# Moving five stores of one batch into the next batch's first product, and the last two stores to another queue

## The chip, the cores and the metric

The kernel runs on one core of one Trainium2 chip. A time is device microseconds of one execution of the whole program, lower is better. The engines of the core are TensorE (matrix products), VectorE, ScalarE, GpSimd and SyncE. SyncE computes nothing here: it only asks for transfers (DMA), as ScalarE and GpSimd also can. Each of these has a queue of its own, worked off in the program's order, and all transfers are carried out by the same 16 DMA engines.

## The reference

Attention with a window and a few sink positions, and behind it a two-part MLP with residuals, for 4 batches of 768 positions:

```python
scores = scale * q @ k.T            # 8 heads of 64; kept: 4 sinks and a causal window of 128
x = softmax(scores) @ v             # heads put side by side: (4, 768, 512)
a1 = alpha1 * x + beta1
u  = x + lam * (w_tok @ a1)         # w_tok mixes the 768 positions
a2 = alpha2 * u + beta2
out = u + lam * (relu(a2 @ w_ch1) @ w_ch2)      # 512 -> 2048 -> 512, float32 out
```

## The kernel before

The positions of a batch are cut into six blocks of 128 rows, called rows 0 to 5 here; a block of 128 x 512 float32 is 256 KB. For each batch the kernel does the attention, the product with `w_tok` (`tok`), a transpose of `u` to float16 by DMA (`uTx`, L919), scale and shift on the transposed halves (L884, L886), the first product with `w_ch1` (`mlp1`, matmuls at L940 and the relu at L946 on ScalarE or L948 on VectorE), and the second product. In batches 1 to 3 the second product is seven half-width products P1 to P7 (`prod`, matmuls at L1057) whose results are added into the rows of `x` by VectorE and GpSimd (L1070, L1088, L1093, L1096). `h_sums` (L998 to L1001) makes their operands.

When the last sum of a row is done, `store` (request at L1076) sends it to the output. In batches 1 and 2 a row goes in one store of 256 KB: rows 3 to 5 after P5, rows 0 to 2 after P3. In batch 3, the last, rows 0 to 2 go in two stores of half the columns, the first half after P2 and the second after P3; rows 3 to 5 go whole.

```python
def store(p, bx, ti, cols, after):
    n_ = (cols.stop - cols.start) // 64
    add(p, {SP: 520, ACT: 550}, lambda e: queue[e].dma_start(out[b, ti * P : (ti + 1) * P, cols], row(bx)[:, cols]),
        after, [bx], lands=(8, 12 * n_ if n_ == 8 else 60))
```

The work is a list of numbered tasks. `add` makes a task; its costs in braces name the engines that may do it. Nothing is planned when the program is built: `emit` goes through `ORDER`, a list of all task numbers, takes each task's engine from the string `ENGINES` (one digit per task: 0 ScalarE, 1 VectorE, 2 TensorE, 3 GpSimd, 4 SyncE), and its buffers from `HOMES`. So `ORDER` is the order of the program, and an engine does its own tasks in that order. An engine runs ahead of the others as far as its data allows: a task's place in `ORDER` only says what it stands behind on its own engine's queue. Requests for transfers of ScalarE and SyncE share eight completion semaphores, which are handed out in turn; a request waits until the one eight before it in the program, which had the same semaphore, has landed. At the end SyncE waits for all transfers (L1329), and the engines meet in a closing barrier. No buffer of batch 2's rows is used again after its store.

The stores from batch 2's end on, in the order of the program:

| Task | Batch, row, columns | Queue | Request before, us |
|---|---|---|---|
| 870 | 2, row 5, all | ScalarE | 217.1 |
| 1093 | 3, row 1, first half | SyncE | 234.0 |
| 864 | 2, row 4, all | SyncE | 234.4 |
| 867 | 2, row 0, all | SyncE | 234.9 |
| 861 | 2, row 3, all | ScalarE | 238.9 |
| 1127 | 3, row 3, all | ScalarE | 245.0 |
| 1088 | 3, row 0, first half | ScalarE | 245.4 |
| 1136 | 3, row 5, all | SyncE | 245.4 |
| 873 | 2, row 1, all | SyncE | 245.7 |
| 876 | 2, row 2, all | SyncE | 246.3 |
| 1096 | 3, row 2, first half | SyncE | 246.8 |
| 1142 | 3, row 2, second half | ScalarE | 247.2 |
| 1130 | 3, row 4, all | ScalarE | 247.6 |
| 1133 | 3, row 0, second half | SyncE | 248.0 |
| 1139 | 3, row 1, second half | SyncE | 249.0 |

Of the kernel before, what the change touches and what calls it, by code (L numbers as in the profile page):

```python
# [77 lines left out]
def kernel(  # L78
# [119 lines left out]
    for r in range(NR):  # L198
# [91 lines left out]
    )  # L290
    ENGINES = (
        "3313134433443333444444444444444433334443111211211212021212021203331121211210210200201210"
# [5 lines left out]
        "2121202111202021202120202011202121212121111121212121212121132111213121421021421421421044"  # L298
        "4400004440443333330404040404040404020201012120101212133201012121312030121213120101212133"
        "2032121312121312104210421040001210421042104000121212120212121212121202120202021202121202"  # L300
        "0202020112120202020212020112021212121211111212121212121213121112131210214214210214214044"
        "4404404404433333304040404043404040202010121203012121312010121213320103212131203012121312"
        "0321213321213121042104210410002104213421341010202021202120212120212020202020212020212120"
        "202020112020212021202020112020210202142141111212121212121211121112131210210214214214210"
    )
    HOMES = (
        "145602340010102001213310200221013302203140101100511203013044215120821000003331a501103130"
# [1026 lines left out]
```

## Time and profile before

| What | Value |
|---|---|
| Median of 3 runs | 254.4 us (254.31 to 255.53) |
| The profiled execution's own time | 254.82 us |
| Its span, first to last instruction | 252.9 us |
| TensorE busy | 245.7 us, 97% of the span |
| VectorE, ScalarE, GpSimd busy | 193.4, 131.4, 107.4 us |
| Mean granted TensorE clock | 0.995 |
| Store requests at L1076 | 13 on SyncE, 8 on ScalarE |

An engine's busy time is a share of the span, an average over stages with different limits. Asking for a transfer is not counted as busy; a row for requests (SPq for SyncE's queue, ACTq for ScalarE's) gives the time of the request itself in ns as smallest, median and largest, and the line on landing gives us from the start of the request until the data has arrived. The profile's rows name a tile without its number, so all rows of all batches are `x`.

### The profile page before, as it was taken

What the parts mean: (1) busy time and instruction counts of PE and PEld (TensorE: products, weight loads), DVE (VectorE), ACT (ScalarE), POOL (GpSimd) and SP (SyncE); (2) the same over time, 40 slices, a digit from 0 to 9 for tenths busy, and PEclk for the clock granted to TensorE, in tenths of its full rate; (3) what the DMA queues carried; (4) which work ended last, traced back from release to release, by engine and by line L of the source; (5) the groups of instructions that cost most, each with busy time, mean ns of one, the idle gap of its engine ahead of it and who ended that gap; (6) DMA issues with size and microseconds to landing.
All of it is one profiled execution on the core that took longest, in us unless ns stands there. A gap on an engine that the chain in (4) does not pass through costs nothing.

```text
span 252.9 us, 5512 instructions
## 1 busy us (share of the span) xinstructions
PE 245.7 (97%) x2167; PEld 160.7 (64%) x2167; DVE 193.4 (76%) x401; ACT 131.4 (52%) x218; POOL 107.4 (42%) x126
## 2 busy tenths in 40 slices
PE   8899999999999999999999999999999999999992
PEld 8654655675555444566777776577577676667882
DVE  6798987778788976688889995677789985039882
ACT  2389935688986025687741435556650234643000
POOL 8618734987866516442772040066562130000010
PEclk9999999999999999999999999999999999999998
DMA  7999999999999997896489274320000131100317
GB/s 214 201 234 292 263 204 306 359 355 285 219 209 231 211 196 166 166 259 141 108 177 178 52 156 128 124 65 0 3 0 3 32 72 23 41 0 3 137 54 268
DMA packets 86129, 38.79 MB, mean 153 GB/s; under 512 B 73540, under 2 KB 80460, under 8 KB 86104
## 3 DMA queue, kind: packets, MB, share of 16 engines
q1 hardware_dynamic: 67120, 28.85, 48.4%
q10 hardware_dynamic: 15240, 6.32, 10.5%
q0 software_dynamic: 3744, 3.28, 8.2%
q8 instruction: 17, 0.28, 0.5%
q14 instruction: 8, 0.07, 0.1%
HBM read 29.91 MB, written 6.29 MB: 143 GB/s over the span
## 4 chain that ended last, share of the span: by engine, by line
PE 90%; ACT 4%; DVE 3%; issue 2%; DVEq 0%; ACTq 0%
PE h L940 32%; PE P L1057 22%; PE tok L860 12%; PE ch L1125 8%; PE pv L726 4%; PE S L625 4%; PE idle L148 2%; PE tp L515 1%; ACT wt L822 1%; ACT E L647 1%; DVE qkT L157 1%; PE S L620 1%; PE tp L512 1%; PE pv L719 1%; DVE lb_b L1175 1%
## 5 line engine op out<-in xcount | busy, mean ns | idle before, releaser
L940 PE MATMUL h<-uT,w1f 128*128 128x384 f16 x512 | 89.3, 326 | 0.1
L940 PEld LDWEIGHTS <-w1f 128*128 128x128 f16 x512 | 48.4, 98 | 31.9 <-issue 2.0
L946 ACT ACTIVATE hT<-h 128x384 f16<-128x384 f32 x77 | 36.7, 492 | 34.4 <-PE h L940 30.6
L948 DVE TENSOR_SCALAR hT<-h 128x384 f16<-128x384 f32 x51 | 27.3, 551 | 23.7 <-PE h L940 23.3
L1057 PEld LDWEIGHTS <-hT 128*128 128x128 f16 x408 | 39.3, 98 | 7.1 <-DVE hT L1000 0.7
L647 ACT ACTIVATE E<-S 128x1024 f16<-128x1024 f32 (+1 forms) x39 | 37.8, 1002 | 6.7 <-PE S L625 5.7
L770 POOL TENSOR_TENSOR tm<-x,la_b 128x512 f32<-128x512 f32 x18 | 24.7, 1372 | 22.2 <-DVE xh L773 12.0
L860 PE MATMUL tok<-xh,wtokT 128*128 128x512 f16 x144 | 33.2, 379 | 0.0
L1057 PE MATMUL P<-w2f,hT 128*128 128x256 f16 x216 | 26.8, 273 | 0.0
L155 ACT CAST u<-x 128x512 f16<-128x512 f32 x17 | 10.3, 616 | 27.3 <-DVE x L867 26.2
L1093 POOL TENSOR_TENSOR x<-x,pt 128x256 f32<-128x256 f32 x4 | 3.9, 963 | 46.0 <-DVE pt L1088 46.0
L1070 DVE TENSOR_TENSOR x<-x,P 128x256 f32<-128x256 f32 x45 | 18.0, 416 | 6.9 <-PE P L1057 6.1
L1057 PE MATMUL P<-w2s,hT 128*128 128x256 f16 x192 | 23.3, 273 | 0.0
L860 PEld LDWEIGHTS <-wtokT 128*128 128x128 f16 x144 | 13.8, 98 | 14.7 <-issue 0.2
L1125 PE MATMUL ch<-w2f,hT 128*128 128x512 f16 x96 | 22.7, 379 | 0.0
L752 DVE TENSOR_TENSOR x<-pv,rec 128x256 f32<-128x256 f32 x48 | 20.4, 424 | 1.6
L155 ACT CAST n<-nat 128x768 f16<-128x768 f32 x20 | 16.2, 830 | 9.2 <-DVE w2s L972 7.2
L867 DVE TENSOR_TENSOR x<-x,tok 128x512 f32<-128x512 f32 x24 | 16.0, 681 | 4.6 <-PE tok L860 4.3
L726 PEld LDWEIGHTS <-E 128*128 128x128 f16 x328 | 15.2, 97 | 4.9 <-issue 1.1
L726 PE MATMUL pv<-vfs,E 128*128 128x65 f16 x328 | 17.7, 194 | 0.0
L587 POOL TENSOR_SCALAR_AFFINE_SELECT E<-E 128x512 f16<-128x512 f16 x12 | 8.8, 756 | 17.9 <-ACT E L647 17.9
L157 POOL CAST vfs<-vnat 128x512 f16<-128x512 f32 x18 | 13.5, 755 | 4.2 <-PE pv L726 4.2
(133 smaller groups left out, 340.2 us busy)
## 6 DMA issues: line engine op xcount, KB each, us to landing
wst_w<-in_moe_w_ch_dram SPq DMA_DIRECT2D x8, 512.0 KB, 7.2
nat<-in_q_dram SPq DMA_DIRECT2D x10, 384.0 KB, 4.5
nat<-in_k_dram SPq DMA_DIRECT2D x10, 384.0 KB, 7.6
vnat<-in_v_dram SPq DMA_DIRECT2D x14, 256.0 KB, 6.2
out_dram<-x SPq DMA_DIRECT2D x11, 256.0 KB, 3.0
out_dram<-x ACTq DMA_DIRECT2D x10, 256.0 KB, 4.0
wtn<-in_moe_w_tok_dram SPq DMA_DIRECT2D x6, 384.0 KB, 6.1
w1f<-in_moe_w_ch_dram POOLq DMA_DIRECT2D x4, 512.0 KB, 10.7
```

The costliest lines, as they stand in the source:

```text
L155: nc.scalar.copy(o, i)
L647: nc.scalar.activation(eT.t, pS.t[:, :, 0 : n * w].rearrange("p e (i w) -> p e i w", i=n), AF.Exp, scale=scale)
L726: nc.tensor.matmul(po.t[:, hl, :], eT.t[:, e_, off + i, c : c + P], vf[j][:, h, :], start=(r < 2 and n == 0), stop=(n == len(parts) - 1 an ...
L752: nc.vector.tensor_mul(bx.t[:, 4 * G : 4 * G + 4, :], po.t[:, :, 0:D], rec.t.to_broadcast([P, 4, D]))
L770: engine[e].tensor_mul(bt.t, bx.t.rearrange("p h d -> p (h d)"), la1_b)
L860: nc.tensor.matmul(bank(), wtokT[:, si, ti * P : (ti + 1) * P], hs[si].t, start=(si == 0), stop=(si == NR - 1))
L940: nc.tensor.matmul(ph.t, w1f[:, c, fi * P : (fi + 1) * P], bu.t[:, c, chk * NTOK : (chk + 1) * NTOK], start=(c == 0), stop=(c == NC - 1))
L946: nc.scalar.activation(bh.t[:, fi, :], ph.t, AF.Relu)
L948: nc.vector.tensor_scalar_max(bh.t[:, fi, :], ph.t, 0.0)
L1057: nc.tensor.matmul(pc.t, hh[:, nt * P : (nt + 1) * P], w(fi), start=(first and n_ == 0), stop=(n_ == HF - 1), skip_group_check=True)
L1070: nc.vector.tensor_add(row(bx)[:, cols], row(bx)[:, cols], pc.t)
L1125: nc.tensor.matmul(pc.t, bh.t[:, fi, nt * P : (nt + 1) * P], w2f[:, fi, :], start=(fi == 0), stop=(fi == NF - 1))
```

## The change

Only `ORDER` and `ENGINES` change. Five stores of batch 2 (864, 867, 861, 873, 876) are taken out of their places among batch 3's second product and put among the tasks of batch 3's first product, around 870, which stays. In the new order the stores of batch 2 read 864, 867, 870, 861, 873, 876, all ahead of 1093. Store 861 (row 3) goes from ScalarE's queue to SyncE's. The program's last two stores, 1133 and 1139, go from SyncE's queue to ScalarE's, where they stand behind 1127, 1088, 1142 and 1130; on SyncE's queue 1093, 1136 and 1096 are left of batch 3. The order of all other tasks among themselves is the same, and so is every other engine digit.

```diff
  1006, 860, 853, 997, 868, 995, 1007, 996, 999, 865, 1008, 858, 857, 1000, 1009,
  862, 869, 866, 874, 1001, 994, 854, 1016, 863, 875, 1040, 1017, 871, 1041, 1038,
  872, 1020, 1039, 1028, 1021, 1011, 1032, 1029, 1013, 1018, 1033, 1024, 1012,
- 1019, 1034, 1010, 1042, 1035, 1025, 1036, 1076, 1037, 1043, 1070, 1077, 870,
- 1074, 1071, 1054, 1075, 1022, 1055, 1060, 1023, 1058, 1061, 1048, 1014, 1049,
- 1059, 1066, 1015, 1044, 1067, 1072, 1045, 1056, 1073, 1026, 1057, 1078, 1068,
- 1079, 1064, 1069, 1046, 1027, 1063, 1052, 1047, 1050, 1053, 1082, 1051, 1062,
- 1084, 1083, 1065, 1030, 1080, 1085, 1101, 1031, 1081, 1091, 1102, 1107, 1092,
- 1097, 1093, 1105, 1108, 864, 1098, 1103, 867, 1106, 1111, 1104, 1113, 1112,
- 1089, 1114, 1115, 1086, 1116, 1090, 861, 1094, 1087, 1109, 1099, 1121, 1100,
- 1117, 1095, 1110, 1125, 1118, 1122, 1134, 1124, 1123, 1126, 1128, 1135, 1127,
- 1088, 1119, 1136, 1120, 1140, 873, 876, 1129, 1131, 1141, 1096, 1142, 1137,
- 1130, 1132, 1133, 1138, 1139,
+ 1019, 864, 1034, 1010, 1042, 1035, 1025, 1036, 867, 1076, 1037, 1043, 1070,
+ 1077, 870, 1074, 1071, 861, 1054, 1075, 1022, 1055, 1060, 1023, 873, 1058, 1061,
+ 1048, 1014, 1049, 1059, 876, 1066, 1015, 1044, 1067, 1072, 1045, 1056, 1073,
+ 1026, 1057, 1078, 1068, 1079, 1064, 1069, 1046, 1027, 1063, 1052, 1047, 1050,
+ 1053, 1082, 1051, 1062, 1084, 1083, 1065, 1030, 1080, 1085, 1101, 1031, 1081,
+ 1091, 1102, 1107, 1092, 1097, 1093, 1105, 1108, 1098, 1103, 1106, 1111, 1104,
+ 1113, 1112, 1089, 1114, 1115, 1086, 1116, 1090, 1094, 1087, 1109, 1099, 1121,
+ 1100, 1117, 1095, 1110, 1125, 1118, 1122, 1134, 1124, 1123, 1126, 1128, 1135,
+ 1127, 1088, 1119, 1136, 1120, 1140, 1129, 1131, 1141, 1096, 1142, 1137, 1130,
+ 1132, 1133, 1138, 1139,
     )
     ENGINES = (
  "3313134433443333444444444444444433334443111211211212021212021203331121211210210200201210"
@@ -298,10 +298,10 @@
  "2121202111202021202120202011202121212121111121212121212121132111213121421021421421421044"
  "4400004440443333330404040404040404020201012120101212133201012121312030121213120101212133"
  "2032121312121312104210421040001210421042104000121212120212121212121202120202021202121202"
- "0202020112120202020212020112021212121211111212121212121213121112131210214214210214214044"
+ "0202020112120202020212020112021212121211111212121212121213121112131214214214210214214044"
  "4404404404433333304040404043404040202010121203012121312010121213320103212131203012121312"
  "0321213321213121042104210410002104213421341010202021202120212120212020202020212020212120"
- "202020112020212021202020112020210202142141111212121212121211121112131210210214214214210"
+ "202020112020212021202020112020210202142141111212121212121211121112131210210210214210210"
     )
     HOMES = (
  "145602340010102001213310200221013302203140101100511203013044215120821000003331a501103130"
```

## The prediction

> **What bounds the kernel now.** I read the page first, then the chain of waits in order of time, then the stretches of the last eight microseconds, then the stores alone.
>
> ```profile
> span 252.9 us, 5512 instructions
> ...
> PE 245.7 (97%) x2167; PEld 160.7 (64%) x2167; DVE 193.4 (76%) x401; ACT 131.4 (52%) x218; POOL 107.4 (42%) x126
> ...
> PE 90%; ACT 4%; DVE 3%; issue 2%; DVEq 0%; ACTq 0%
> ```
>
> TensorE is busy for 97% of the span. The chain of waits from 196 us on shows that in both places that the change touches nothing but TensorE is on the path:
>
> ```profile
> 210.53 18.85 PE h L940 x116
> ...
> 231.78 16.61 PE P L1057 x152
> 248.39 0.02 issue
> 248.41 0.42 DVE x L1070
> ```
>
> The chain ends with the last sum on VectorE at 248.41 + 0.42 = 248.83. The span ends at 252.9. What lies in these 4.1 us is no engine's work, so the stores must be read by themselves (the last one, then the program's closing instructions, L1329):
>
> ```profile
> L1076 SPq DMA_DIRECT2D out_dram<-x x1: 965/965/965, 249.0 to 249.0; - x1
> DMA to landing us min/median/max: 2.7/2.7/2.7
> ...
> L1329 SPq EVENT_SEMAPHORE  x11: 17/28/28, 250.0 to 252.8; - x11
> ...
> L1329 SPq DRAIN  x3: 7/7/13, 252.1 to 252.4; - x3
> ```
>
> The last store is asked for at 249.0, 0.15 us after its data, and lands 2.7 us later, at 251.7. SyncE waits for the landings one by one (11 waits from 250.0), drains at 252.1, and the span ends 1.2 us after the last landing. So the tail is: data ready 248.83, +0.15 to the request, +2.7 to the landing, +1.2 to close. Why 2.7 is in the stretches (the last two numbers of a row are the busy share of the 16 DMA engines and GB/s; the number before them is the granted clock):
>
> ```profile
> 245.00:246.00 1.00, 1.00 (x11) 0.90 (x10) 1.00 (x3) 0.00 (x0) 0.23 (x1) 1.00 0.14 49
> 246.00:247.00 1.00, 1.00 (x11) 0.90 (x10) 0.90 (x3) 0.00 (x0) 0.00 (x0) 1.00 1.03 381
> 247.00:248.00 1.00, 1.00 (x12) 0.89 (x11) 0.58 (x2) 0.00 (x0) 0.00 (x0) 1.00 1.02 361
> 248.00:249.00 1.00, 0.38 (x4) 0.09 (x1) 0.42 (x1) 0.00 (x0) 0.00 (x0) 1.00 1.03 379
> 249.00:250.00 1.00, 0.00 (x0) 0.00 (x0) 0.00 (x0) 0.00 (x0) 0.00 (x0) 1.00 1.03 349
> 250.00:251.00 1.00, 0.00 (x0) 0.00 (x0) 0.00 (x0) 0.00 (x0) 0.00 (x0) 0.73 1.04 358
> 251.00:252.00 1.00, 0.00 (x0) 0.00 (x0) 0.00 (x0) 0.00 (x0) 0.00 (x0) 0.50 0.27 90
> ```
>
> The DMA engines are full (1.02 to 1.04) from 246 to 251, at a mean of (381 + 361 + 379 + 349 + 358) / 5 = 366 GB/s. The seven rows add up to 1.97 MB, which is ten stores: five of 256 KB (0.262 MB) and five of half a row (0.131 MB). Two of the five large ones are batch 2's rows 1 and 2. The last store's data waits behind a backlog. Without one, a 256 KB store looks like this (the store of batch 2's row 3, asked for at 238.9 with nothing else in flight):
>
> ```profile
> L1076 ACTq DMA_DIRECT2D out_dram<-x x1: 338/338/338, 238.9 to 238.9; - x1
> DMA to landing us min/median/max: 2.0/2.0/2.0
> ...
> 239.50:240.50 1.00, 1.00 (x12) 0.90 (x10) 0.74 (x2) 0.00 (x0) 0.00 (x0) 1.00 0.70 262
> ```
>
> It lands after 2.0 us, of which its data takes 0.7. Half of the data takes 0.131 / 0.366 = 0.36 us less, so I estimate 1.65 us for a half store on free engines.
>
> **The change, part one: five stores of batch 2 move forward.** In the tail this removes two of SyncE's requests (rows 1 and 2, 0.524 MB) from in front of the last stores. At 366 GB/s that is 1.43 us of backlog. Not all of it can be had, since the last store's data is not ready before 248.83. What is left, 1.44 MB: the first four stores (0.79 MB) are through at about 245.9 + 2.1 = 248.0, and the other four are asked for from 247.2 on, about as fast as they move. The last landing time therefore falls from 2.7 towards 1.65: a gain between 0.7 (if it lands as the lone 256 KB store, 2.0) and 1.05. The other three, rows 4 and 0 (asked for from 234.4 on) and row 3 (238.9), leave stretches in which nobody waits for them: nothing there.
>
> Where they go: SyncE's queue holds six transposes up to 206.24 + 2.51 = 208.75 and then nothing until 234.0, so the five run there as soon as their sums are done, before the place in the program at which they stand.
>
> ```profile
> 206.24 2.51 SPq L919 DMA_TRANSPOSE uT<-u  x2
> ...
> 208.60 0.75 DVE L1070 TENSOR_TENSOR x<-x,P 128x256 f32<-128x256 f32 x2
> 210.57 0.42 DVE L1070 TENSOR_TENSOR x<-x,P 128x256 f32<-128x256 f32 x1 [1.22 <-PE P L1057]
> 212.26 1.29 ACT L884 ACTIVATE uT<-uT,ab 128x384 f16<-128x384 f16 x2
> 214.40 0.37 DVE L886 TENSOR_SCALAR uT<-uT,ab 128x384 f16<-128x384 f16 x1
> ...
> 209.00:209.75 0.75, 0.75 (x8) 0.52 (x6) 0.35 (x2) 0.54 (x2) 0.00 (x0) 1.00 0.59 113
> 209.75:210.50 0.75, 0.75 (x9) 0.65 (x7) 0.00 (x0) 0.44 (x1) 0.00 (x0) 1.00 0.00 0
> ...
> L1076 SPq DMA_DIRECT2D out_dram<-x x3: 333/426/535, 234.0 to 234.9; - x3
> ```
>
> Row 4's sum ends near 209.0, the sums of rows 0, 3 and 2 are there by 209.35, row 1's at 210.99. Three stores in a row took SyncE 0.33, 0.43 and 0.54 us, so five take at most 2.7 us of an idle queue. Their 1.31 MB move from about 209.8 to 214. Who could suffer: the last transposes, but their data is through by 209.75 (the row after that shows 0), and they stand ahead on the same queue. If the stores did hold them up, ScalarE and VectorE read them from 212.26 on, VectorE's last of these sums ends at 214.77, and TensorE first needs it after 44 matmuls of the first half, 36 of them behind 210.53 at 18.85 / 116 = 0.1625 us: 216.4. That cover is 1.6 us; if it is gone, each further microsecond of delay is a microsecond of the time. TensorE beside a full DMA is not slower: 246:247 shows it busy 1.00 of 1.00 at a share of 1.03, with the same 11 matmuls as 245:246 at 0.14. Cost: 0, bounds 0 and +0.3.
>
> **Part two: queues.** Row 3's store leaves ScalarE's queue: 0.34 us before an idle stretch, worth 0. The last two stores (second halves of rows 0 and 1) go from SyncE to ScalarE, behind row 2's second half and the whole row 4:
>
> ```profile
> 246.38 0.78 DVE L1070 TENSOR_TENSOR x<-x,P 128x256 f32<-128x256 f32 x2
> 247.54 0.42 DVE L1070 TENSOR_TENSOR x<-x,P 128x256 f32<-128x256 f32 x1 [0.38 <-PE P L1057]
> ...
> L1076 SPq DMA_DIRECT2D out_dram<-x x4: 333/502/969, 245.4 to 246.8; - x4
> ...
> DMA to landing us min/median/max: 2.5/2.5/2.5
> ...
> L1076 SPq DMA_DIRECT2D out_dram<-x x2: 901/935/969, 246.8 to 248.0; - x2
> L1076 ACTq DMA_DIRECT2D out_dram<-x x2: 338/530/721, 247.2 to 247.6; - x2
> DMA to landing us min/median/max: 3.4/3.4/3.4
> ```
>
> ScalarE is now done issuing at 247.57 + 0.72 = 248.29. Row 0's half is ready at 247.96 and would start at 248.34 (SyncE started it at 248.0): 0.3 later, but it is not the last. It then takes 0.34 (an idle queue) to 0.72 (ScalarE's second in a row), or 0.97 if it meets what SyncE met under the backlog. Row 1's half starts at 248.87 at the earliest, at 249.1 with 0.72, at 249.36 with 0.97; today 249.0. I take 249.0, between the first two, since the backlog that goes with 0.97 is what part one removes. So the queue change alone is worth about 0, bounds -0.15 and +0.35, and SyncE's queue after part one would have been as free.
>
> A request also waits for the landing of the one that stands eight before it in the program. Today, for the last two, these are the stores of 245.0 and 245.4, which landed by about 247.8 (2.5 us), before the data of 247.96. After the change they are batch 2's row 2 and the store of 234.0, long landed: worth 0 either way.
>
> A rule against it: the Trainium skill, "DMA: Bandwidth & Descriptors", section "Issuing engines are not separate DMA queues", holds that requests from several engines run on the same 16 DMA engines and that spreading them saves only the sequencer's time. The trace agrees (share 1.03 with both queues asking). By it the queue change is worth at most the 0.15 us between data and request.
>
> **The sum**, against the profiled run (254.82 us, of which 252.9 are span and 1.9 lie around it). Request at 249.0 as now; landing 1.65 plus 0.1 for a request right behind another (0.43 against 0.33 above), 1.75 instead of 2.7; closing 1.2 as now. Gain 0.95, rounded to 1.0. Span 251.9, profiled run 253.8. The median of the runs shown is 254.4 (254.31 to 255.53), 0.4 under the profiled run, so I forecast 253.4. Best end: 248.87 + 1.65 + 1.2 = 251.7, a gain of 1.2. Worst: 249.36 + 2.7 + 1.2 = 253.3, a loss of 0.4.
>
> One price stands on a page only: the Trainium skill, "DMA: Bandwidth & Descriptors", section "Anatomy of one DMA — SWDGE (gpsimd) path", fits 2.0 us plus the bytes over 436 GB/s for requests of GpSimd, which is 2.3 us for a half store and 2.6 for a whole one. The trace shows 2.0 for a whole one on these queues, so the trace decides; by the page's price the gain would be 0.4.
>
> **The rivals.** A change of 0.5%, 1.27 us, is about what a measurement of this kernel can tell from none.
>
> *Faster by over 0.5%.* The best end above is a gain of 1.2, so this needs both issues on ScalarE at 0.34 us and a half store that lands in under 1.6. For it: the backlog is gone, and an idle queue did issue in 0.34. Against: every second store in a row took 0.43 to 0.72. It gives 253.1.
>
> *The landing doesn't shrink.* Four stores follow one another on one queue, each issue takes 0.72 to 0.97, and the last one still lands after 2.3 to 2.7. For it: row 4's store on ScalarE took 3.4 us to land. Against: that one stood in the backlog. It gives 249.2 + 2.5 + 1.2 = 252.9: no change, 254.4 (254.0 to 254.8).
>
> *Slower.* The five stores fill the DMA engines from 209.8 to 214 while the transposes, the second half's scale-and-shift and TensorE's next product are on their way. If the transposes were served only after the stores, they would land 1.31 / 0.366 = 3.6 us late, at about 213.6 instead of 210; VectorE's last sum would then end at about 215.2, still ahead of 216.4. It decides from a delay of 4.8 us on, and to lose more than 0.5% on top of the gain of 1.0 it takes 7.1 us. Against it is that the transposes come first on their queue. It would give 254.4 - 1.0 + 2.3 = 255.7.
>
> **How the numbers follow.** Forecast (gain 0.6 to 1.2): 0.62. Faster than 0.5%: 0.2. No shrinking: 0.13. Slower: 0.05. The last two of the same sign as "same" add up: faster 0.2, same 0.75, slower 0.05. The forecast's own range is 253.2 to 253.8. The range reaches down to the floor less the 0.4 us by which runs of one kernel lie apart around their median, 252.7, and up to the worst end, 254.7.
>
> **What would show it.** Right: five requests on SyncE between 209 and 213, and DMA share near 1 in 210:214; TensorE busy 7.00 of 7.00 in 209:216; the share below 1 in part of 247:250; the last request at 248.9 to 249.1, on ScalarE, landing after 1.7 to 2.0; the last sum on VectorE still at 248.8; 1.2 us from the last landing to the end. Wrong: a gap on TensorE around 212 to 217, issues of 0.9 us on ScalarE after 248, or a closing part longer than 1.2 us because ScalarE now drains last.

## The result, and the profile after

The changed kernel took 253.3 us (median of 7 runs, 253.09 to 254.45) against 254.78 us of the kernel before (7 runs, 254.31 to 255.53). The ratio is 0.9946, 95% interval 0.9925 to 0.9967: 1.4 us less, somewhere between 0.8 and 1.9. Forecast was 1.0 less and 253.4 us.

The profiled execution took 253.3 us with a span of 251.5. First the page and the end of the chain of waits, which answer to the first lines shown of before:

```profile
span 251.5 us, 5513 instructions
...
PE 245.2 (98%) x2167; PEld 160.2 (64%) x2167; DVE 193.7 (77%) x401; ACT 131.5 (52%) x218; POOL 107.9 (43%) x126
```

```profile
210.10 18.85 PE h L940 x116
...
231.34 16.61 PE P L1057 x152
247.95 0.02 issue
247.98 0.42 DVE x L1070
```

Batch 3's products take 18.85 and 16.61 us as before, to the digit. The last sum ends at 247.98 + 0.42 = 248.40, which is 0.43 us earlier than before; this lead is already there at 210.10 (before: 210.53), and VectorE shows about as much, 0.46, near the start (first before, then the changed kernel):

```profile
15.71 0.96 DVE L157 COPY qkT<-tp 128x768 f16<-128x768 f16 x1 [0.36 <-PE tp L512]
```

```profile
15.25 0.96 DVE L157 COPY qkT<-tp 128x768 f16<-128x768 f16 x1
```

That is 190 us ahead of anything that was changed, so the span's 1.44 us must be split: 0.43 come from there, and the rest from the **tail**, by which I mean the time from the end of the last sum to the end of the span. It fell from 4.07 us (248.83 to 252.90) to 3.06 (248.40 to 251.46). From the start of the piece of 18.85 us to the last sum it is 38.3 us in both (210.53 to 248.83 and 210.10 to 248.40). The last store, and SyncE's part in the closing of the changed kernel:

```profile
L1076 ACTq DMA_DIRECT2D out_dram<-x x1: 339/339/339, 248.4 to 248.4; - x1
...
DMA to landing us min/median/max: 1.9/1.9/1.9
```

```profile
L1329 SPq EVENT_SEMAPHORE  x10: 17/28/28, 249.0 to 251.4; - x10
...
L1329 SPq DRAIN  x3: 7/7/13, 250.6 to 250.9; - x3
```

The request leaves at 248.4 with its data, where it left 0.15 late before; it lands 1.9 us later instead of 2.7; the span ends 1.2 us after that landing, as before. The stretches show the early slot in the first row and then the tail (the last two numbers are the share of the DMA engines and GB/s):

```profile
209.00:216.00 7.00, 7.00 (x48) 4.45 (x46) 2.58 (x6) 3.65 (x9) 0.00 (x0) 1.00 0.52 190
245.00:246.00 1.00, 1.00 (x11) 0.90 (x10) 0.90 (x3) 0.00 (x0) 0.00 (x0) 1.00 0.56 207
246.00:247.00 1.00, 1.00 (x11) 0.89 (x10) 0.72 (x2) 0.00 (x0) 0.00 (x0) 1.00 0.87 310
247.00:248.00 1.00, 0.94 (x9) 0.59 (x7) 0.45 (x2) 0.00 (x0) 0.00 (x0) 1.00 1.02 342
248.00:249.00 1.00, 0.00 (x0) 0.00 (x0) 0.40 (x1) 0.00 (x0) 0.00 (x0) 1.00 1.02 366
249.00:250.00 1.00, 0.00 (x0) 0.00 (x0) 0.00 (x0) 0.00 (x0) 0.00 (x0) 1.00 0.66 217
250.00:251.00 1.00, 0.00 (x0) 0.00 (x0) 0.00 (x0) 0.00 (x0) 0.00 (x0) 1.00 0.00 0
```

The bytes of 209:216 went from 0.1 MB (15 GB/s over 7 us) to 1.33 MB (190 GB/s), the five stores, and TensorE is busy 7.00 of 7.00 as before. From 245 on the rows add up to 1.44 MB instead of 1.97, and the DMA engines are done in 249:250, a good microsecond sooner against the last sum.

### The profile page after: what moved, and what is told of

The parts are those of the page before. It is cut to its first block, busy times and chain, and to the rows that moved or that the text cites. A ratio compares the mean times of both kernels' runs of the same rounds, so it can differ in the third digit from the quotient of the medians.

```text
span 251.5 us, 5513 instructions
## 1 busy us (share of the span) xinstructions
PE 245.2 (98%) x2167; PEld 160.2 (64%) x2167; DVE 193.7 (77%) x401; ACT 131.5 (52%) x218; POOL 107.9 (43%) x126
## 4 chain that ended last, share of the span: by engine, by line
PE 90%; ACT 4%; DVE 3%; issue 1%; DVEq 0%; ACTq 0%
PE h L940 32%; PE P L1057 22%; PE tok L860 12%; PE ch L1125 8%; PE pv L726 4%; PE S L625 4%; PE idle L148 2%; PE tp L515 1%; ACT wt L822 1%; ACT E L647 1%; DVE qkT L157 1%; PE S L620 1%; PE tp L512 1%; PE pv L719 1%; DVE lb_b L1175 1%
```

## The experiments

Two theories were set against each other. **Backlog:** the bytes asked for ahead of the last store set when it lands, since the DMA engines have to move them first. **Queue:** what helped is that the last two stores leave SyncE. All are judged by the tail as well as by the time, since what lies ahead of the change moves the whole span by more than half a microsecond from run to run, and the tail does not contain it. The last column of the table is the ratio of the runs to those of the kernel before, with its 95% interval; the columns before it come from one profile of each kernel. Before again and the lone store have one run each, and so no ratio.

| Kernel | MB in the tail | Last two stores on | Last sum ends, us | Span, us | Tail, us | Ratio |
|---|---|---|---|---|---|---|
| before | 1.97 | SyncE | 248.83 | 252.9 | 4.07 | |
| before again | 1.97 | SyncE | 248.74 | 252.9 | 4.14 | |
| queue change alone | 1.97 | ScalarE | 248.41 | 252.7 | 4.28 | 0.9999 (0.9985 to 1.0013) |
| five stores late | 2.75 | SyncE | 249.20 | 255.3 | 6.13 | 1.0078 (1.0053 to 1.0103) |
| changed kernel | 1.44 | ScalarE | 248.40 | 251.5 | 3.06 | 0.9946 (0.9925 to 0.9967) |
| changed kernel again | 1.44 | ScalarE | 249.51 | 252.5 | 3.00 | 0.9968 (0.9953 to 0.9983) |
| moves alone | 1.44 | SyncE | 248.19 | 251.1 | 2.91 | 0.9933 (0.9914 to 0.9951) |
| two rows moved | 1.44 | SyncE | 249.28 | 252.2 | 2.91 | 0.9949 (0.9931 to 0.9968) |
| early halves | 1.18 | SyncE | 249.41 | 252.3 | 2.90 | 0.9960 (0.9942 to 0.9978) |
| lone store | 0.13 | SyncE | 248.80 | 251.6 | 2.84 | |

**Moves alone.** The changed kernel with the last two stores back on SyncE (from here on the differences between kernels are given in short, by the tasks concerned):

```diff
 ENGINES, by task                     # 0 ScalarE, 4 SyncE
-    1133: 0, 1139: 0
+    1133: 4, 1139: 4
```

> The change without its queue part: the five stores of batch 2 moved, the last two stores left on SyncE. Measured by the tail, from the end of the last sum on VectorE to the end of the span: before 4.07 us (248.83 to 252.90), changed kernel 3.06 us (248.40 to 251.46). Backlog theory (the bytes in front of the last store set the tail): 3.0 to 3.2 us, the whole gain, ratio to before about 0.995. Queue theory (what helped is that the last two stores are asked for on ScalarE): 3.7 us or more, ratio 0.998 or more.

Its last store and the end of its chain:

```profile
L1076 SPq DMA_DIRECT2D out_dram<-x x1: 332/332/332, 248.2 to 248.2; - x1
...
DMA to landing us min/median/max: 1.7/1.7/1.7
```

```profile
231.14 16.61 PE P L1057 x152
247.75 0.02 issue
247.77 0.42 DVE x L1070
```

The request leaves 248.2, at the end of the last sum (247.77 + 0.42 = 248.19), and lands after 1.7 us. The tail is 2.91: the whole gain is in the moves, as the backlog theory has it. The tail is even shorter than the 3.0 to 3.2 that was expected, and 0.1 to 0.15 shorter than that of the changed kernel.

**Queue change alone.**

```diff
 ENGINES of before, by task
-    1133: 4, 1139: 4
+    1133: 0, 1139: 0
```

> The queue part alone: the five stores stay where they were, the last two stores go to ScalarE. Backlog theory: the same 1.97 MB stand in the tail, which stays 3.9 to 4.2 us; ratio 0.999 to 1.001. Queue theory: 3.1 to 3.5 us, ratio about 0.996.

```profile
L1076 ACTq DMA_DIRECT2D out_dram<-x x2: 920/936/953, 247.7 to 248.7; - x2
...
DMA to landing us min/median/max: 2.8/2.8/2.8
```

No gain: ratio 0.9999, tail 4.28, slightly over the range that was given (3.9 to 4.2). Both requests now take 0.92 to 0.95 us on ScalarE, as they did on SyncE (0.90 and 0.97), the last one leaves 0.3 us after its data and lands after 2.8. So the slow requests go with the backlog and not with the queue: with 1.97 MB in the tail the last two take 0.90 to 1.01 us on either queue, with 1.44 MB 0.33 to 0.42. The queue theory falls.

**Five stores late**, the opposite of the change:

```diff
 ORDER of before
-    1093, 1105, 1108, 864, 1098, 1103, 867, ...  1090, 861, ...  1120, 1140, 873, 876, ...
+    1093, 1105, 1108, 1098, 1103, ...  1090, ...  1120, 1140, 864, 867, 861, 873, 876, ...
 ENGINES, by task
-    861: 0
+    861: 4
```

> The opposite of the change: before, with the stores of batch 2's rows 4, 0 and 3 pushed back as well, to just ahead of rows 1 and 2 on SyncE's queue, so that all five stand in the tail (0.786 MB more than before). Backlog theory: tail longer by 0.786 / 0.366 = 2.15 us, 6.2 us, time 2.1 us over before. If only the number of requests on SyncE counted (three more at 0.5 us, part of it while it waits anyway): 1.0 us longer or less, 5.1 us.

The stretches of its tail:

```profile
247.00:248.00 1.00, 1.00 (x11) 0.90 (x10) 0.62 (x3) 0.00 (x0) 0.00 (x0) 1.00 1.03 374
...
252.00:253.00 1.00, 0.00 (x0) 0.00 (x0) 0.00 (x0) 0.00 (x0) 0.00 (x0) 0.50 1.02 359
253.00:254.00 1.00, 0.00 (x0) 0.00 (x0) 0.00 (x0) 0.00 (x0) 0.00 (x0) 0.50 0.73 240
```

Its last requests:

```profile
L1076 SPq DMA_DIRECT2D out_dram<-x x5: 394/792/1192, 248.3 to 252.1; - x5
...
DMA to landing us min/median/max: 2.0/2.5/2.9
```

The DMA engines stay full two microseconds longer. The tail is 6.13, which is 2.06 longer for 0.786 MB, or 381 GB/s; the ratio 1.0078 is 2.0 us. But the wait shows at another place than in the kernel before. The last store lands only 2.0 us after its request; the request itself leaves at 252.1, 2.9 us after the last sum, because those ahead of it on SyncE's queue took up to 1.19 us each. So this run alone does not tell bytes from requests: three more requests at 0.4 to 1.2 us each, where 0.5 was expected, would also give about 2 us. For the bytes speak the DMA engines, which are full from 247 to 253, and the queue change alone, which takes two requests off SyncE and leaves the tail as long.

**Before again.** The same kernel as before.

> The kernel before, once more, for its profile. In the changed kernel all engines run 0.43 us ahead of before from 16 us on, long before anything that was changed. If that is scatter of the loads at the start, this profile of before again has its last sum on VectorE anywhere from 248.2 to 249.2 us, with a tail of 4.0 to 4.2. If the change made it, it is at 248.7 to 248.9 here, and at 248.3 to 248.5 in the kernel with the moves alone.

Tail 4.14, last sum at 248.74. Over all ten profiles the last sum ends anywhere from 248.19 to 249.51: the earliest and the latest both belong to kernels with the moves, and those without lie between (248.41 to 249.20). From the start of the 18.85 us of `h` to the last sum it is 38.3 us in all ten, so the whole difference lies ahead of that. The 0.43 us lead of the first pair of profiles is scatter of what comes before, and no gain of the change. Where a profile moved against the first one, it was mostly within the first 16 us, as above, and for the kernel with two rows moved near 97 us (0.55 us late from there on).

**Two rows moved**, from the kernel before:

```diff
 ORDER of before
-    1120, 1140, 873, 876, 1129, ...
+    1120, 1140, 1129, ...
-    1060, 1023, 1058, 1061, 1048, 1014, 1049, 1059, 1066, ...
+    1060, 1023, 873, 1058, 1061, 1048, 1014, 1049, 1059, 876, 1066, ...
```

> Before, with only batch 2's rows 1 and 2 moved into batch 3's first product (the two stores that stood in the tail); rows 4, 0 and 3 stay at 234 to 239, and the last two stores stay on SyncE. Backlog theory: the other three moves are worth nothing, so the tail is as short as with all five moved and the last two on SyncE (2.91 us): 2.85 to 3.1, ratio 0.993 to 0.997. If each moved store had its share, two of five would leave it at 3.6 us.

Tail 2.91, ratio 0.9949, the same as with all five moved. Of the five moves, the two stores that stood in the tail are the whole effect; rows 4, 0 and 3 at 234 to 239 were in nobody's way.

**Lone store.** Of batch 3's stores only row 1's two halves are made; the outputs of rows 0, 2, 3, 4 and 5 of batch 3 are missing.

```diff
 for i in order:
-    t = self.tasks[i]
+    t = (a task that does nothing) if i in (1088, 1096, 1127, 1130, 1133, 1136, 1142) else self.tasks[i]
 ENGINES, by task
-    1133: 0, 1139: 0
+    1133: 4, 1139: 4
```

> The price that the prediction had to estimate: a half store on free DMA engines. The moves with the last two stores on SyncE, and of batch 3's stores only the first half and the second half of row 1 are made (rows 0, 2, 3, 4 and 5 of batch 3 are not stored). The last store then stands alone. Estimate: it lands 1.65 us after its request, tail 0.03 + 1.65 + 1.17 = 2.85 us. With all eight other stores of the tail in front of it the tail was 2.91 (last two on SyncE) and 3.06 (changed kernel). If 1.65 is too long, the tail here is 2.7 or less and a backlog is still left in the changed kernel; if half a row costs as much as a whole one (2.0), 3.2.

```profile
231.75 16.61 PE P L1057 x152
248.36 0.03 issue
248.38 0.42 DVE x L1070
```

```profile
L1076 SPq DMA_DIRECT2D out_dram<-x x1: 332/332/332, 248.8 to 248.8; - x1
```

Tail 2.84. The profile gives no landing for this request. Less 0.03 to the request and 1.1 to 1.2 to close, the half store landed after 1.6 to 1.7 us: the estimate of 1.65 holds, and this is the floor, the shortest tail that a last store of this size leaves. The moves alone (2.91, eight stores in the tail, the last one included) stand 0.07 above it with 1.3 MB more in flight.

**Early halves**, a version that goes on from the moves:

```diff
 ORDER of the changed kernel
-    1086, 1116, 1090, 1094, 1087, 1109, ... 1117, 1095, 1110, ... 1127, 1088, ... 1131, 1141, 1096, 1142, 1137, 1130, 1132, ...
+    1086, 1116, 1090, 1094, 1087, 1088, 1109, ... 1117, 1095, 1096, 1110, ... 1127, ... 1129, 1130, 1131, 1141, 1142, 1137, 1132, ...
 ENGINES, by task
-    1088: 0, 1133: 0, 1139: 0
+    1088: 4, 1133: 4, 1139: 4
```

> A version that goes on: the five moves, the last two stores on SyncE, the first halves of batch 3's rows 0 and 2 asked for on SyncE as soon as they are summed (240 to 243 instead of 244.7 to 246), and row 4's store ahead of row 2's second half on ScalarE. 0.262 MB less in the tail. Backlog theory with a floor of a lone store: the tail is at its floor, 2.75 to 2.9 us, 0.15 to 0.3 under the changed kernel; ratio to before 0.992 to 0.995. If the backlog still ruled, another 0.262 / 0.366 = 0.7 us would go: tail 2.3.

```profile
L1076 SPq DMA_DIRECT2D out_dram<-x x2: 332/332/332, 248.6 to 249.4; - x2
...
DMA to landing us min/median/max: 1.7/1.7/1.7
```

Tail 2.90, no shorter than with the moves alone: with 1.7 us the last store lands as a lone one does, and fewer bytes in front of it help no more. The ratio, 0.9960, is outside the 0.992 to 0.995 that was expected. Its interval overlaps with those of the moves alone and of two rows moved; the ratio itself is no better than theirs.

**Changed kernel again.**

> The changed kernel once more, beside the others on the same chip. Tail 3.0 to 3.2 us again; the last sum on VectorE anywhere from 248.2 to 249.2 us; ratio to before 0.994 to 0.997. If ScalarE's queue holds the last two stores back, its tail stays 0.1 to 0.2 over that of the kernel with the moves alone (2.91); if that was scatter, both ranges overlap.

```profile
L1076 ACTq DMA_DIRECT2D out_dram<-x x3: 339/411/465, 248.2 to 249.5; - x3
...
DMA to landing us min/median/max: 1.8/2.1/2.5
```

Tail 3.00, ratio 0.9968: 0.8 us faster, between 0.4 and 1.2. The last sum, at 249.51, ended later than the 248.2 to 249.2 that was expected. Its tail and that of the first profile (3.00, 3.06) both lie above the three kernels with the same or fewer bytes and the last two stores on SyncE (2.90 to 2.91). The difference is in the landing (1.8 and 1.9 against 1.7); the request leaves with its data in all five. Two profiles against three make a cost of ScalarE's queue of about 0.1 us likely. The times leave it open: the interval of this run starts at 0.9953, just above the end of that of the moves alone (0.9951), but the interval of the changed kernel's first measurement overlaps with both, and the two ratios of the changed kernel differ by 0.0022 between themselves.

## Why the prediction was right

*The bound.* Right. TensorE was not touched in either place (18.85 and 16.61 us in all ten profiles), and the tail was the only part that changed (the 38.3 us ahead of it are the same in all ten).

*Part one.* The mechanism was right. Its gain was put at 0.7 to 1.05 in the landing alone, plus what of the 0.15 us late request comes back; the moves alone took 4.07 to 2.91, 1.16, which is both ends together: landing 2.7 to 1.7, request from 0.15 late to none. That 1.43 us of backlog would not all be had was shown twice: by the lone store's 2.84 and by the early halves' 2.90. The estimate took half of the data for half of the time on the DMA engines; the lone half store kept them busy for 0.39 us (shares 0.32 and 0.07 of two stretches of 1 us), the lone whole one for 0.70.

*Part two.* Forecast 0, bounds -0.15 and +0.35. Measured +0.1 to +0.2 in the tail (4.28 against 4.07 and 4.14; 3.00 and 3.06 against 2.91), and nothing in the time of the queue change alone. The rule of the Trainium skill, "DMA: Bandwidth & Descriptors", section "Issuing engines are not separate DMA queues", that another queue saves no more than the time to ask, agrees with these runs: the queue change alone is 0.9999.

*The sum.* Two terms were off and nearly cancel, which is luck. The last request was put at 249.0, 0.17 us after its data, because ScalarE's requests were given up to 0.72 us; the last four took 0.34, 0.47, 0.42 and 0.34, so it left at once. The landing was put at 1.75 and took 1.9. The DMA engines are still full until 249 (1.02 in 247:249); the share below 1 in part of 247:250 that was forecast came only with the last bytes (0.66 in 249:250). That is not yet the cause, since with the moves alone they are full in 248:249 too (1.00) and the last store lands after 1.7; why it takes longer on ScalarE stays open. Request and landing together: 1.92 forecast, about 1.9 measured. Closing was 1.2 both times. Gain of the tail 0.95 forecast, 1.0 measured.

*The time.* The ratio 0.9946 is 1.4 us, just over the 0.5% that I called the limit of what can be told, and 0.9968 is 0.8 us, under it. The tails say 1.0 to 1.1, 0.4%. The remaining 0.4 of the first figure lies within its interval (0.8 to 1.9), and no trace shows a gain ahead of the tail. So the case with a chance of 0.62 is most likely what happened, and the first measurement landed on the far side of the line by scatter. That 253.3 came so close to the forecast 253.4 is luck in part: the forecast started from a median of 254.4 of 3 runs, the 7 runs of before have 254.78, and the gain measured with them is larger by about as much.

*The rivals.* The landing did shrink (1.9, and 1.7 with SyncE). Of the faster rival's two conditions, short requests on ScalarE came about (0.42 and 0.34), but the last half store never landed in under 1.6 us. For the slower one, the five requests ran at 208.6 to 211.7 in the idle part of SyncE's queue. The DMA engines were busy for 0.74 of 210:214, not near 1 as forecast. The scale-and-shift that reads the transposes ran as early as before against TensorE (changed kernel):

```profile
211.82 1.29 ACT L884 ACTIVATE uT<-uT,ab 128x384 f16<-128x384 f16 x2
213.21 0.37 DVE L886 TENSOR_SCALAR uT<-uT,ab 128x384 f16<-128x384 f16 x1
213.97 0.37 DVE L886 TENSOR_SCALAR uT<-uT,ab 128x384 f16<-128x384 f16 x1
```

211.82 and 213.97 against 212.26 and 214.40 is the lead of 0.43 to 0.44 us from before and nothing else. As far as these rows show, the cover of 1.6 us was not used at all; the landing of the last transpose itself is not in the profile.

*The page's price* of 2.3 us for a half store, an estimate from the fit for requests of GpSimd in the Trainium skill, "DMA: Bandwidth & Descriptors", section "Anatomy of one DMA — SWDGE (gpsimd) path", does not carry over to these queues. With 1.44 MB or less in the tail, the last half store landed after 1.7 us when SyncE asked for it, and after 1.8 to 1.9 when ScalarE did.

## What to carry to other kernels

At the end of a program the chain of waits stops at the last computation; read on from there with the stretches, the time at which the last store is asked for, and its landing; a backlog can show in either of the two. If the DMA engines are full when the last result is ready, every byte asked for before it that could have gone earlier costs its share (2.06 us for 0.786 MB here), until the last store lands as fast as a lone one; from there on fewer bytes gained nothing here (2.90 against 2.91), and which engine asks mattered by 0.1 to 0.2 us at most. Where a gain is smaller than the scatter of the whole time, compare the stretch that the change can reach, here the tail, and take what lies ahead of it out of the comparison.

## What the runs showed of the hardware that I had not expected

A request can be slow although the DMA engines are not full all the time (0.56 in 245:246 of the changed kernel). In it the first half of row 0 took ScalarE 1.48 us to ask for and row 2's took SyncE 1.13, when only two whole rows, and for the second of them row 0's half, were in front:

```profile
L1076 ACTq DMA_DIRECT2D out_dram<-x x5: 339/416/1480, 244.6 to 247.7; - x5
L1076 SPq DMA_DIRECT2D out_dram<-x x2: 332/733/1134, 244.9 to 245.3; - x2
```

The two slow requests stand on different queues and end together, at 246.44 and 246.45. In seven of the ten profiles the second request of ScalarE and the second of SyncE after 244 us end within 0.02 us of each other, so what holds them up seems to be common to both queues. Nothing waits behind them here; whether such a request would hold up an engine that has work behind it, no run here shows. In the early slot one of SyncE's five took 1.03 us where I had allowed 0.54:

```profile
L1076 SPq DMA_DIRECT2D out_dram<-x x5: 333/431/1031, 208.6 to 211.7; - x5
```

What makes a single request take that long stays open; no experiment here was made for it.
